# Weight chunks' loads in the opening wait for a one-word VectorE write to their buffer

## The chip, the cores and the metric

The kernel runs on one core of a Trainium2 chip. The metric is the device time of one execution in microseconds (us). A core has five engines that run their own instruction streams in order and wait for each other by semaphores: TensorE (PE; its weight loads are PEld), VectorE (DVE), ScalarE (ACT), GpSimd (POOL) and SyncE (SP), which here does nothing but issue transfers (DMAs).

## The reference

Three stages follow one another, all in float32. First a gated linear attention over 4 batches, 8 heads, 768 steps and 48 channels; then two MLPs over the 3072 tokens of 384 channels, each with a hidden layer of 2048.

```python
f = 1.0 / (1.0 + np.exp(-f_logit))
for t in range(S):
    state = f[:, :, t, :, None] * state + np.einsum('bhd,bhe->bhde', k[:, :, t], v[:, :, t])
    y[:, :, t] = np.einsum('bhd,bhde->bhe', q[:, :, t], state)
x = y.transpose(0, 2, 1, 3).reshape(B * S, H * D)
h = x @ moe_w_in;  g = np.maximum(h, 0.0) ** 2;  x = g @ moe_w_out
h = x @ moe2_w_in; g = h * np.tanh(softplus(h)); out = g @ moe2_w_out
```

## The kernel before

**Attention** is cut into 24 units, i = 0 to 23 (12 chunks of 64 steps, two pairs of batches each). A unit loads its gate logits, k and q (`load_j` and `load_f`, or `load_f` alone), and its v (`load_v`, two transfers), and passes through `v_min`, `a_exp`, `a_ln`, `v_scan`, `a_dq`, `a_dk`, `v_q`, `v_k`, `m_a`, `m_t`, `v_mask`, `a_kn`, `m_y`, `m_u`, `a_y`, `m_x`, `v_s`, `a_x`, `v_x`. The letter ahead of the underscore is the engine: `m` TensorE, `v` VectorE, `a` ScalarE, `load` SyncE. Four units make one block of 512 tokens for the MLPs.

**The first MLP** takes its hidden layer in 16 chunks. For block b and chunk fc, numbered i = 16 b + fc, `do_l1 i` makes the hidden values (9 matmuls, line 333), `act_a i` (ScalarE) and `act_b i` (VectorE, line 357) square and split them into a high part `gh` and a low part `gl`, and `do_l2 i` multiplies them back (9 matmuls, line 344). The second of the 9 matmuls of `do_l2` reads `gl`.

**Weights** are stored as 64-bit words and converted on the chip. Chunk fc of the first MLP (both of its matrices, 768 KB) is loaded by `load_w fc` into a buffer of its own (tag `w_fc`), and then goes through six steps: `w_abs` (ScalarE, line 251, the first to read the buffer), `w_shift` (VectorE, line 255), `w_top` (258), `w_low` (261), `w_hi` (ScalarE, 278) and `w_lo` (VectorE, 283). `do_l1 fc` needs what `w_hi` and `w_lo` wrote. The buffers of chunks 12 to 15 first serve as the inputs of units 5 to 2.

**The order** of the first part, up to the middle of `do_l1 18`, is written out in the string `START`; later steps are placed by the functions `unit`, `put` and `run`. Each engine runs its own steps in the order in which `START` names them, so the string is five queues in one. Warm-up matmuls (`m_warm`) keep TensorE busy in the opening. SyncE's queue before is, with j for `load_j`, f for `load_f`, v for `load_v`, w for `load_w`:

```
j0 j1 j2 j3 f0 f1 v0 w0 v1 f2 v2 f3 v3 w1 w2 w3 w4 f5 w5 w6 v4 w7 w8 w9 w11 f4 v5 f7 w10 f6 v7 w14 w12 w13 w15 v8 v6 f9 f8 v10 v9 f10
```

A transfer waits for the steps that still use its destination; the buffers of chunks 0 to 11 have no earlier user, so before the change their loads wait for nothing but their turn.

Of the kernel before, what the change touches and what calls it, by code (L numbers as in the profile page):

```python
# [35 lines left out]
START = """
m_warm 14; load_j 0; v_min 0; a_exp 0; load_j 1; load_j 2; load_j 3; a_ln 0; v_min 1; a_exp 1; v_scan 0; a_ln 1;
load_f 0; load_f 1; v_min 2; v_scan 1; a_dq 0; v_min 3; a_dk 0; v_k 0; a_exp 2; a_dq 1; v_q 0 1; v_q 0 0; a_dk 1;
load_v 0; load_w 0; a_ln 2; a_exp 3; eye_kn 0; load_v 1; load_f 2; m_t 0; m_warm 2; v_end 1; v_k 1; v_q 1 1;
load_v 2; v_scan 2; a_ln 3; load_f 3; v_end 0; v_q 1 0; m_a 0; m_warm 5; v_scan 3; v_mask 0 0; w_abs 0; v_mask 0 1;  # L40
m_a 1; m_warm 4; a_dq 2; a_dk 2; v_mask 1 1; load_v 3; a_dq 3; v_mask 1 0; m_y 0; a_kn 0; load_w 1; w_shift 0;
a_dk 3; v_q 2 0; m_t 1; m_warm 2; w_top 0; eye_kn 1; a_y 0; v_q 2 1; load_w 2; m_y 1; m_warm 3; a_y 1; v_q 3 0;
v_k 3; v_k 2; v_q 3 1; w_low 0; m_x 0; a_x 0; m_u 0; a_kn 1; v_s 0 0; m_a 2; w_abs 1; v_x 0; load_w 3; v_mask 2 0;
m_u 1; v_s 1 0; v_s 0 1; w_shift 1; m_a 3; m_t 3; v_mask 2 1; w_hi 0; a_kn 3; m_t 2; m_warm 1; m_y 2; a_kn 2;
v_s 1 1; v_mask 3 1; v_mask 3 0; m_x 1; m_warm 1; m_y 3; m_warm 1; w_lo 0; w_top 1; load_w 4; w_abs 2; a_x 1; v_x 1;
a_y 2; w_shift 2; m_x 2; load_f 5; a_y 3; w_low 1; a_x 2; load_w 5; m_x 3; m_warm 6; load_w 6; v_end 3; a_x 3; v_x 3;
v_x 2; w_top 2; do_l1 0; w_hi 1; w_abs 3; load_v 4; w_lo 1; w_low 2; do_l1 1; w_abs 4; w_shift 3; v_min 5; w_hi 2;
load_w 7; w_top 3; a_exp 5; w_lo 2; w_shift 4; m_u 3; load_w 8; w_low 3; act_a 0; act_b 0; w_abs 5; w_top 4; w_hi 3;
w_shift 5; load_w 9; do_l1 2; act_a 1; w_lo 3; w_low 4; w_hi 4; act_b 1; load_w 11; w_top 5; w_lo 4; w_low 5;
v_s 3 0; do_l2 0; do_l1 3; do_l2 1; act_a 2; act_b 2; do_l1 4; w_abs 6; w_hi 5; w_abs 7; w_shift 6; w_lo 5; w_top 6;  # L50
do_l2 2; act_a 3; w_abs 8; w_shift 7; w_low 6; load_f 4; a_ln 5; w_hi 6; w_top 7; act_b 3; v_s 3 1; act_a 4; w_lo 6;
w_abs 9; do_l1 5; do_l2 3; w_low 7; w_hi 7; load_v 5; act_b 4; w_shift 8; load_f 7; act_a 5; w_shift 9; load_w 10;
do_l1 6; w_top 8; load_f 6; do_l2 4; v_end 2; w_lo 7; w_top 9; w_low 8; act_b 5; act_a 6; w_hi 8; w_abs 11; v_min 4;
v_scan 5; w_lo 8; load_v 7; do_l1 7; w_low 9; load_w 14; a_exp 4; do_l2 5; a_ln 4; act_b 6; a_dq 5; w_hi 9; a_dk 5;
v_q 5 1; w_abs 10; w_lo 9; v_scan 4; do_l1 8; act_a 7; do_l2 6; v_k 5; a_dq 4; v_q 5 0; act_a 8; do_l1 9; a_dk 4;
w_shift 10; act_b 7; w_top 10; v_q 4 1; m_t 5; v_min 6; w_shift 11; v_k 4; act_a 9; act_b 8; m_a 5; load_w 12;
do_l2 7; v_min 7; m_u 2; v_q 4 0; do_l2 8; w_low 10; a_kn 5; m_a 4; w_top 11; m_t 4; a_exp 7; v_mask 5 0; w_hi 10;
a_ln 7; w_lo 10; v_end 5; v_end 4; w_low 11; act_b 9; w_abs 12; w_hi 11; w_shift 12; v_mask 5 1; w_top 12; do_l1 10;
do_l2 9; w_lo 11; act_a 10; do_l1 11; w_low 12; load_w 13; w_hi 12; w_abs 13; act_b 10; do_l2 10; v_mask 4 1;
w_lo 12; v_s 2 0; v_s 2 1; do_l1 12; act_a 11; w_shift 13; v_mask 4 0; w_abs 14; a_exp 6; act_b 11; m_y 5; a_ln 6;  # L60
w_top 13; w_shift 14; a_kn 4; do_l2 11; w_low 13; v_scan 6; w_hi 13; m_y 4; w_lo 13; a_y 5; act_a 12; do_l1 13;
v_scan 7; w_top 14; a_dq 7; act_b 12; a_dk 7; load_w 15; w_low 14; v_q 7 0; m_u 5; v_s 5 0; v_k 7; a_dq 6; v_q 7 1;
do_l2 12; act_a 13; m_u 4; a_dk 6; m_a 7; act_b 13; v_s 4 0; v_q 6 1; w_hi 14; v_q 6 0; do_l2 13; v_s 5 1; load_v 8;
v_k 6; a_y 4; v_s 4 1; v_mask 7 1; m_t 7; a_kn 7; w_abs 15; v_mask 7 0; m_a 6; v_mask 6 1; m_t 6; m_y 7; v_mask 6 0;
m_x 5; a_kn 6; load_v 6; a_x 5; m_x 4; m_y 6; a_y 7; a_x 4; w_lo 14; w_shift 15; do_l1 14; v_end 7; a_y 6; w_top 15;
w_low 15; v_x 5; load_f 9; w_hi 15; v_x 4; load_f 8; v_end 6; m_u 7; m_x 6; act_a 14; w_lo 15; m_u 6; v_s 7 0;
v_min 8; v_s 7 1; a_exp 8; v_min 9; do_l1 15; a_ln 8; m_x 7; a_x 6; act_b 14; a_x 7; v_scan 8; v_x 6; a_dq 8; v_x 7;
v_s 6 1; do_l2 14; a_dk 8; a_exp 9; v_s 6 0; v_k 8; act_a 15; v_q 8 0; act_b 15; a_ln 9; do_l1 16; v_scan 9; m_t 8;
v_end 8; act_a 16; load_v 10; do_l1 17; a_dq 9; v_q 8 1; v_q 9 0; v_end 9; a_dk 9; load_v 9; do_l2 15; a_kn 8;
v_q 9 1; do_l1 18; act_b 16; m_a 8; v_mask 8 1; v_mask 8 0; do_l2 16; m_y 8; m_u 8; act_a 17; a_y 8; load_f 10;  # L70
y_dma 8; act_b 17; v_k 9; v_s 8 0; v_s 8 1
"""
# [871 lines left out]
```

## Time and profile before

| | |
|---|---|
| runs | 898.8, 900.05, 900.1 us; median 900.05 us |
| profiled execution | 899.7 us, of which the span from first to last instruction is 897.9 us |
| granted TensorE clock | 0.998 of full speed |
| PE busy | 884.8 us, 99% of the span |
| DVE busy | 675.9 us, 75% |
| ACT busy | 618.5 us, 69% |
| first matmuls of `do_l1 0` without a gap | from 35.52 us |

Times in the rows below are us from the start of the span. The 1.8 us between span and execution lie outside the instructions. Granted clock 1.00 is the higher of the two levels, 2.4 GHz.

### The profile page before, as it was taken

Reading aid. Unit: us, or ns where it says so; the run is one execution under the profiler, and the core shown is the slowest. Engines: PE = TensorE matmul, PEld = TensorE weight load, DVE = VectorE, ACT = ScalarE, POOL = GpSimd, SP = SyncE. Lnnn points to the kernel's source line nnn. Section 1 sums busy time; section 2 is a strip of 40 time slices with the busy share of each in tenths; the row PEclk is TensorE's granted clock in tenths of the full one; section 3 lists DMA queues with packets and bytes.
Section 4 is the critical chain, followed back from the end, with each engine's and each line's share of the span. In section 5 each row is a group of like instructions: output and inputs, shape, how many; then the busy total and the mean of one; then the engine's idle time right before and its main releaser. Section 6 shows DMA issues by size and latency. Waiting matters only on the chain.

```text
span 897.9 us, 15329 instructions
## 1 busy us (share of the span) xinstructions
PE 884.8 (99%) x5927; PEld 726.5 (81%) x5927; DVE 675.9 (75%) x1146; ACT 618.5 (69%) x1131; POOL 5.3 (1%) x21
## 2 busy tenths in 40 slices
PE   8899999999999999999999999999999999999997
PEld 8788888888787887888888888888888888888885
DVE  8999976776778777772222788888788888888785
ACT  7898776876787678764544566666666676666664
POOL 2000000000000000000000000000000000000000
PEclk9999999999999999999999999999999999999999
DMA  9972223454536465622453200200100100200001
GB/s 244 351 172 106 82 89 100 152 186 157 187 126 228 135 195 165 221 101 81 175 200 118 71 0 1 72 1 0 71 1 1 71 0 1 72 1 0 36 1 38
DMA packets 34287, 89.93 MB, mean 100 GB/s; under 512 B 5216, under 2 KB 11360, under 8 KB 34208
## 3 DMA queue, kind: packets, MB, share of 16 engines
q1 hardware_dynamic: 34208, 88.89, 30.8%
q8 instruction: 48, 0.79, 0.4%
q14 instruction: 31, 0.25, 0.1%
HBM read 63.70 MB, written 22.02 MB: 95 GB/s over the span
## 4 chain that ended last, share of the span: by engine, by line
PE 87%; ACT 4%; DVE 3%; DMA 3%; SPq 2%; issue 1%; ACTq 0%
PE h L333 40%; PE a L344 40%; PE y L525 2%; DMA r<-in_w_dram 1%; DMA ax<-ay 1%; PE tr L486 1%; PE aq L471 1%; ACT r L716 1%; PE uq L538 1%; DMA sr<-in_w_dram 1%; PE u L543 1%; PE at L476 1%; PE y L518 0%; DMA vs<-in_vv_dram 0%; ACT r L715 0%
## 5 line engine op out<-in xcount | busy, mean ns | idle before, releaser
L333 PE MATMUL h<-x,w 128*128 128x512 f32 x1728 | 425.3, 390 | 0.4 <-DVE x L606 0.3
L344 PE MATMUL a<-gh,w 128*128 128x512 f32 x1146 | 388.3, 394 | 0.0
L333 PEld LDWEIGHTS h<-x,w 128*128 128x128 f32 x1728 | 323.6, 188 | 69.9 <-DVE x L606 1.0
L344 PEld LDWEIGHTS a<-gh,w 128*128 128x128 f32 x1146 | 215.2, 188 | 46.1
L344 PE MATMUL a<-gl,w 128*128 128x512 f32 x573 | 223.7, 391 | 0.0
L782 ACT ACTIVATE e<-e 128x512 f32<-128x512 f32 x95 | 60.1, 632 | 117.6 <-DVE e L781 117.6
L344 PEld LDWEIGHTS a<-gl,w 128*128 128x128 f32 x573 | 107.7, 188 | 22.0 <-DVE gl L357 0.7
L357 DVE TENSOR_TENSOR gl<-r,gh 128x512 fp32r<-128x512 f32 x96 | 65.8, 685 | 78.4 <-ACT gh L352 78.1
L781 DVE TENSOR_SCALAR e<-h 128x512 f32<-128x512 f32 x95 | 65.7, 692 | 60.7 <-PE h L333 58.1
L715 ACT ACTIVATE r<-h 128x512 f32<-128x512 f32 x96 | 56.6, 590 | 50.4 <-PE h L333 49.9
L776 ACT ACTIVATE r<-u,cst 128x512 f32<-128x512 f32 x94 | 67.9, 722 | 8.7 <-DVE u L790 2.7
L790 DVE SCALAR_TENSOR_TENSOR u<-e 128x512 f32<-128x512 f32 x95 | 65.9, 693 | 10.1 <-ACT e L782 0.7
L357 DVE TENSOR_TENSOR gl<-g,gh 128x512 fp32r<-128x512 f32 x95 | 65.7, 692 | 0.0
L778 DVE TENSOR_TENSOR e<-h,u 128x512 f32<-128x512 f32 x94 | 64.3, 684 | 0.0
L785 DVE TENSOR_TENSOR g<-e,r 128x512 f32<-128x512 f32 x94 | 64.2, 683 | 0.0
L716 ACT ACTIVATE r<-r 128x512 f32<-128x512 f32 x96 | 60.7, 632 | 3.1
L352 ACT ACTIVATE gh<-r 128x512 fp32r<-128x512 f32 x96 | 60.7, 632 | 3.1
L352 ACT ACTIVATE gh<-g 128x512 fp32r<-128x512 f32 x95 | 60.1, 633 | 3.1 <-DVE g L809 0.8
L777 ACT ACTIVATE r<-r 128x512 f32<-128x512 f32 x94 | 59.5, 633 | 3.0
L606 DVE TENSOR_TENSOR x<-ax,x 128x384 fp32r<-128x384 f32 x16 | 8.9, 555 | 35.3 <-ACT x L602 35.3
L602 ACT ACTIVATE x<-ax 128x384 fp32r<-128x384 f32 x16 | 8.4, 525 | 37.0 <-DMA ax<-ay 36.8
L508 ACT ACTIVATE kn<-tr 64x192 f32<-64x192 f32 x88 | 28.4, 322 | 6.1 <-PE tr L486 5.2
(120 smaller groups left out, 730.5 us busy)
## 6 DMA issues: line engine op xcount, KB each, us to landing
r<-in_w_dram SPq DMA_DIRECT2D x16, 768.0 KB, 11.7
sr<-in_w_dram SPq DMA_DIRECT2D x32, 384.0 KB, 3.5
w2d<-sw SPq DMA_DIRECT2D x32, 384.0 KB, 3.2
w<-w2d SPq DMA_DIRECT2D x32, 384.0 KB, 3.6
in<-in_qkf_dram SPq DMA_DIRECT2D x18, 672.0 KB, 5.8
vs<-in_vv_dram SPq DMA_DIRECT2D x48, 96.0 KB, 5.6
x2d<-ot SPq DMA_DIRECT2D x18, 256.0 KB, 2.2
x<-x2d SPq DMA_DIRECT2D x6, 768.0 KB, 5.1
```

The lines of the kernel that those rows point to most:

```text
L333: T.matmul(out=ps, lhsT=w[:, k * 128:(k + 1) * 128], rhs=x[:, s, k], start=(i == 0), stop=(i == 8))
L344: T.matmul(out=acc[m], lhsT=w[:, m * 128:(m + 1) * 128], rhs=gx, start=(fc == 0 and i == 0), stop=(fc == FC - 1 and i == 2))
L352: A.activation(out=gh, in_=g, func=AF.Copy)
L357: V.tensor_tensor(out=gl, in0=g, in1=gh.bitcast(F32), op=ALU.subtract)
L716: A.activation(out=r, in_=r, func=AF.Square)
L776: A.activation(out=r, in_=u, func=AF.Ln, bias=two)
L777: A.activation(out=r, in_=r, func=AF.Exp, scale=-1.0)
L778: V.tensor_tensor(out=e, in0=hp, in1=u, op=ALU.mult)
L781: V.tensor_scalar(out=e2, in0=ps, scalar1=20.0, scalar2=None, op0=ALU.min)
L782: A.activation(out=e2, in_=e2, func=AF.Exp)
L785: V.tensor_tensor(out=g, in0=e, in1=r, op=ALU.mult)
L790: V.scalar_tensor_tensor(out=u2, in0=e2, scalar=2.0, in1=e2, op0=ALU.add, op1=ALU.mult)
```

## The change

A new step `v_gate fc` allocates the buffer of chunk fc and writes one 32-bit word to it with a VectorE memset. `load_w fc` then takes that buffer, and since it writes over the same word it has to wait for the memset, that is, for VectorE to have come to that place of its queue. Chunks 1 to 11, 14 and 15 get a gate (13 memsets); 0, 12 and 13 don't. `START` is replaced. The queues of VectorE, ScalarE and TensorE name the same steps in the same order as before, but for the gates. SyncE's queue is another from `w1` on:

```
j0 j1 j2 j3 f0 f1 v0 w0 v1 f2 v2 f3 v3 w1 f5 w2 v4 w3 w4 f4 v5 f7 w5 f6 w6 w7 v7 w8 w9 w11 w10 w12 w14 w13 w15 v8 v6 f9 f8 v10 v9 f10
```

The places of the gates in VectorE's queue: gate 1 behind `v_scan 2`, 2 behind `w_shift 0`, 3 behind `w_low 0`, 4 behind `v_mask 2 0`, 5 behind `v_mask 3 0`, 6 behind `w_low 2`, 7 behind `w_top 3`, 8 behind `w_low 3`, 9 behind `act_b 1`, 11 behind `w_shift 7`, 10 behind `w_low 7`, 14 behind `w_top 11`, 15 behind `v_scan 7`. Five stand ahead of the last VectorE step that `do_l1 0` needs (`v_x 2`), eight ahead of `w_lo 3`, ten ahead of `act_b 3`.

```diff
 START = """
-m_warm 14; load_j 0; v_min 0; a_exp 0; load_j 1; load_j 2; load_j 3; a_ln 0; v_min 1; a_exp 1; v_scan 0; a_ln 1;
-load_f 0; load_f 1; v_min 2; v_scan 1; a_dq 0; v_min 3; a_dk 0; v_k 0; a_exp 2; a_dq 1; v_q 0 1; v_q 0 0; a_dk 1;
-load_v 0; load_w 0; a_ln 2; a_exp 3; eye_kn 0; load_v 1; load_f 2; m_t 0; m_warm 2; v_end 1; v_k 1; v_q 1 1;
...
-y_dma 8; act_b 17; v_k 9; v_s 8 0; v_s 8 1
+m_warm 14; load_j 0; load_j 1; load_j 2; load_j 3; load_f 0; v_min 0; load_f 1; a_exp 0; load_v 0; v_min 1; a_ln 0;
...
+eye_kn 0; v_q 1 1; v_scan 2; m_warm 5; v_end 1; a_ln 3; v_gate 1; load_w 1; v_q 1 0; v_end 0; v_scan 3; load_f 5;
+m_a 1; w_abs 0; v_mask 0 0; m_warm 4; a_dq 2; v_mask 0 1; a_dk 2; v_mask 1 1; m_y 0; a_dq 3; v_mask 1 0; a_kn 0;
+m_t 1; w_shift 0; m_warm 2; v_gate 2; load_w 2; v_q 2 0; a_dk 3; w_top 0; m_y 1; eye_kn 1; v_q 2 1; m_warm 3; a_y 0;
+v_q 3 0; a_y 1; v_k 3; m_x 0; m_u 0; v_k 2; a_x 0; a_kn 1; v_q 3 1; m_a 2; load_v 4; w_low 0; v_gate 3; load_w 3;
+m_u 1; v_s 0 0; w_abs 1; v_x 0; m_a 3; v_mask 2 0; v_gate 4; load_w 4; w_hi 0; v_s 1 0; m_t 3; v_s 0 1; load_f 4;
+a_kn 3; w_shift 1; m_t 2; load_v 5; v_mask 2 1; m_warm 1; v_s 1 1; m_y 2; a_kn 2; load_f 7; v_mask 3 1; m_x 1;
+v_mask 3 0; v_gate 5; load_w 5; m_warm 1; w_abs 2; load_f 6; w_lo 0; m_y 3; a_x 1; a_y 2; w_top 1; m_warm 1; a_y 3;
...
     def load_w(fc):
-        t = wp.tile([128, 2 * DM, 2], U32, tag=f"w_{fc}", name=f"r_{fc}", bufs=1)
+        t = raw.get(fc) or wp.tile([128, 2 * DM, 2], U32, tag=f"w_{fc}", name=f"r_{fc}", bufs=1)
         nc.sync.dma_start(out=t.rearrange("p c w -> p (c w)"), in_=w1[fc].bitcast(U32))
         raw[fc] = t
+
+    def v_gate(fc):
+        raw[fc] = wp.tile([128, 2 * DM, 2], U32, tag=f"w_{fc}", name=f"r_{fc}", bufs=1)
+        V.memset(raw[fc][0:1, 0:1, 0:1].bitcast(F32), 0.0)
```

## Rows read from the trace of the kernel before

**Rows 1.** The page: the chain that ended last, shares of the span.
```profile
PE 87%; ACT 4%; DVE 3%; DMA 3%; SPq 2%; issue 1%; ACTq 0%
```
**Rows 2.** Windows: length, busy time by engine, clock, DMA share, GB/s moved.
```profile
9.60:35.50 25.90, 22.58 (x409) 20.06 (x408) 25.45 (x39) 20.29 (x52) 0.00 (x0) 1.00 1.03 306
...
45.60:61.00 15.40, 15.40 (x68) 12.44 (x67) 15.31 (x23) 15.05 (x28) 0.00 (x0) 1.00 0.98 237
61.00:71.00 10.00, 10.00 (x45) 8.29 (x45) 9.94 (x14) 9.20 (x17) 0.00 (x0) 1.00 0.01 6
```
**Rows 3.** Groups by line, 16 to 140 us: w_abs of 15 chunks.
```profile
L251 ACT ACTIVATE wbit<-r 128x768 f32<-128x768 f32 x15 | 13.6, 906 | 0.9 <-DVE w L283 0.9
```
**Rows 4.** TensorE's timeline: matmuls of do_l1 0 and 1, gl's weight load in do_l2 3.
```profile
35.52 4.13 PE L333 MATMUL h<-x,w 128*128 128x512 f32 x17 [0.27 <-DVE x L606]
...
55.22 0.19 PEld L344 LDWEIGHTS a<-gl,w 128*128 128x128 f32 x1 [0.40 <-DVE gl L357]
```
**Rows 5.** VectorE's timeline: v_k 0; w_shift 0; act_b 0, w_top 4, w_shift 5, w_lo 3; act_b 3.
```profile
9.61 0.69 DVE L453 TENSOR_TENSOR in<-in,es 112x512 f32<-112x512 f32 x1 [1.09 <-DMA in<-in_qkf_dram]
...
18.57 0.54 DVE L255 TENSOR_SCALAR wbit<-wbit 128x768 uint32<-128x768 uint32 x1
...
41.88 0.67 DVE L357 TENSOR_TENSOR gl<-r,gh 128x512 fp32r<-128x512 f32 x1
42.48 0.94 DVE L258 SCALAR_TENSOR_TENSOR wbit<-r,wbit 128x768 uint32<-128x768 uint32 x1
43.35 0.54 DVE L255 TENSOR_SCALAR wbit<-wbit 128x768 uint32<-128x768 uint32 x1
43.82 0.94 DVE L283 SCALAR_TENSOR_TENSOR w<-wbit,w 128x768 fp32r<-128x768 f32 x1
...
54.48 0.69 DVE L357 TENSOR_TENSOR gl<-r,gh 128x512 fp32r<-128x512 f32 x1
```
**Rows 6.** w_low by its tile, 16 to 140 us: minimum, median, maximum in ns.
```profile
L261 DVE SCALAR_TENSOR_TENSOR wbit<-r,wbit x16: 939/942/959, 23.9 to 110.1; 128x768 uint32<-128x768 uint32 x16
```
**Rows 7.** VectorE's timeline at the start: memsets of one word in each partition.
```profile
1.70 0.06 DVE L622 MEMSET cst<- 112x1 f32 x1
1.82 0.06 DVE L623 MEMSET cst<- 32x1 f32 x1
```
**Rows 8.** SyncE's timeline, issues of w1, w4, f5, w5 and f4.
```profile
15.34 0.58 SPq L242 DMA_DIRECT2D r<-in_w_dram  x1
...
17.99 0.43 SPq L242 DMA_DIRECT2D r<-in_w_dram  x1
18.47 0.43 SPq L407 DMA_DIRECT2D early<-in_qkf_dram  x1
...
20.86 0.33 SPq L242 DMA_DIRECT2D r<-in_w_dram  x1
...
34.91 0.38 SPq L407 DMA_DIRECT2D early<-in_qkf_dram  x1
```
**Rows 9.** DMA issues of those stretches, w1, w4, f5, w5: us to landing last.
```profile
r<-in_w_dram SPq DMA_DIRECT2D x1, 768.0 KB, 7.8
...
r<-in_w_dram SPq DMA_DIRECT2D x1, 768.0 KB, 12.2
early<-in_qkf_dram SPq DMA_DIRECT2D x1, 672.0 KB, 14.8
...
r<-in_w_dram SPq DMA_DIRECT2D x1, 768.0 KB, 14.0
```
**Rows 10.** ScalarE's timeline: w_abs 5, w_hi 3, w_abs 7 and w_abs 8.
```profile
41.26 0.90 ACT L251 ACTIVATE wbit<-r 128x768 f32<-128x768 f32 x1
...
42.14 0.85 ACT L278 ACTIVATE w<-wbit 128x768 fp32r<-128x768 f32 x1
...
49.85 0.90 ACT L251 ACTIVATE wbit<-r 128x768 f32<-128x768 f32 x1
...
52.57 0.91 ACT L251 ACTIVATE wbit<-r 128x768 f32<-128x768 f32 x1
```

More of the change, by code (lines that the diff above doesn't have):

```diff
@@ L36 @@
 START = """
-m_warm 14; load_j 0; v_min 0; a_exp 0; load_j 1; load_j 2; load_j 3; a_ln 0; v_min 1; a_exp 1; v_scan 0; a_ln 1;
-load_f 0; load_f 1; v_min 2; v_scan 1; a_dq 0; v_min 3; a_dk 0; v_k 0; a_exp 2; a_dq 1; v_q 0 1; v_q 0 0; a_dk 1;
-load_v 0; load_w 0; a_ln 2; a_exp 3; eye_kn 0; load_v 1; load_f 2; m_t 0; m_warm 2; v_end 1; v_k 1; v_q 1 1;
-load_v 2; v_scan 2; a_ln 3; load_f 3; v_end 0; v_q 1 0; m_a 0; m_warm 5; v_scan 3; v_mask 0 0; w_abs 0; v_mask 0 1;
-m_a 1; m_warm 4; a_dq 2; a_dk 2; v_mask 1 1; load_v 3; a_dq 3; v_mask 1 0; m_y 0; a_kn 0; load_w 1; w_shift 0;
@@ L42 @@
[L42 to L70, printed above, removed]
-y_dma 8; act_b 17; v_k 9; v_s 8 0; v_s 8 1
+m_warm 14; load_j 0; load_j 1; load_j 2; load_j 3; load_f 0; v_min 0; load_f 1; a_exp 0; load_v 0; v_min 1; a_ln 0;
@@ new lines @@
+a_exp 1; v_scan 0; load_w 0; a_ln 1; load_v 1; v_min 2; a_dq 0; v_scan 1; load_f 2; a_dk 0; load_v 2; a_exp 2;
+v_min 3; v_k 0; a_dq 1; v_q 0 1; load_f 3; a_dk 1; m_t 0; v_q 0 0; a_ln 2; m_warm 2; load_v 3; v_k 1; a_exp 3; m_a 0;
+eye_kn 0; v_q 1 1; v_scan 2; m_warm 5; v_end 1; a_ln 3; v_gate 1; load_w 1; v_q 1 0; v_end 0; v_scan 3; load_f 5;
+m_a 1; w_abs 0; v_mask 0 0; m_warm 4; a_dq 2; v_mask 0 1; a_dk 2; v_mask 1 1; m_y 0; a_dq 3; v_mask 1 0; a_kn 0;
+m_t 1; w_shift 0; m_warm 2; v_gate 2; load_w 2; v_q 2 0; a_dk 3; w_top 0; m_y 1; eye_kn 1; v_q 2 1; m_warm 3; a_y 0;
@@ new lines @@
+v_q 3 0; a_y 1; v_k 3; m_x 0; m_u 0; v_k 2; a_x 0; a_kn 1; v_q 3 1; m_a 2; load_v 4; w_low 0; v_gate 3; load_w 3;
+m_u 1; v_s 0 0; w_abs 1; v_x 0; m_a 3; v_mask 2 0; v_gate 4; load_w 4; w_hi 0; v_s 1 0; m_t 3; v_s 0 1; load_f 4;
+a_kn 3; w_shift 1; m_t 2; load_v 5; v_mask 2 1; m_warm 1; v_s 1 1; m_y 2; a_kn 2; load_f 7; v_mask 3 1; m_x 1;
+v_mask 3 0; v_gate 5; load_w 5; m_warm 1; w_abs 2; load_f 6; w_lo 0; m_y 3; a_x 1; a_y 2; w_top 1; m_warm 1; a_y 3;
+m_x 2; v_x 1; w_shift 2; a_x 2; m_x 3; m_warm 6; v_end 3; w_low 1; a_x 3; v_x 3; w_hi 1; v_x 2; w_top 2; w_abs 3;
@@ new lines @@
+do_l1 0; w_lo 1; w_low 2; w_abs 4; v_gate 6; load_w 6; do_l1 1; w_shift 3; w_hi 2; v_min 5; w_top 3; a_exp 5;
+v_gate 7; load_w 7; act_a 0; w_lo 2; m_u 3; w_shift 4; do_l1 2; w_low 3; load_v 7; w_abs 5; v_gate 8; load_w 8;
+act_b 0; w_hi 3; w_top 4; do_l2 0; act_a 1; w_shift 5; w_lo 3; w_low 4; do_l1 3; act_b 1; w_hi 4; v_gate 9; load_w 9;
+w_top 5; act_a 2; do_l2 1; w_lo 4; w_low 5; w_abs 6; v_s 3 0; do_l1 4; w_hi 5; act_b 2; w_shift 6; w_abs 7; w_lo 5;
+act_a 3; do_l2 2; w_top 6; w_shift 7; v_gate 11; load_w 11; w_low 6; w_abs 8; do_l1 5; w_top 7; a_ln 5; w_hi 6;
@@ new lines @@
+act_b 3; v_s 3 1; do_l2 3; act_a 4; w_lo 6; w_low 7; v_gate 10; load_w 10; w_abs 9; do_l1 6; act_b 4; w_hi 7;
+w_shift 8; w_shift 9; act_a 5; w_top 8; do_l2 4; w_lo 7; v_end 2; w_top 9; act_a 6; do_l1 7; w_low 8; act_b 5;
+w_hi 8; v_min 4; v_scan 5; w_abs 11; do_l2 5; a_exp 4; w_lo 8; a_ln 4; w_low 9; do_l1 8; a_dq 5; act_b 6; w_hi 9;
+v_q 5 1; a_dk 5; w_lo 9; do_l2 6; w_abs 10; v_scan 4; act_a 7; v_k 5; do_l1 9; v_q 5 0; a_dq 4; w_shift 10; act_a 8;
+act_b 7; m_t 5; w_top 10; m_a 5; v_q 4 1; a_dk 4; v_min 6; do_l2 7; act_a 9; load_w 12; w_shift 11; v_k 4; act_b 8;
@@ new lines @@
+a_kn 5; v_min 7; m_u 2; v_q 4 0; w_low 10; do_l2 8; a_exp 7; w_top 11; w_hi 10; v_gate 14; load_w 14; v_mask 5 0;
+a_ln 7; m_a 4; w_lo 10; v_end 5; v_end 4; w_abs 12; w_low 11; m_t 4; do_l1 10; load_w 13; act_b 9; w_hi 11;
+w_shift 12; v_mask 5 1; do_l2 9; w_top 12; act_a 10; w_lo 11; w_low 12; do_l1 11; act_b 10; w_hi 12; v_mask 4 1;
+w_abs 13; w_lo 12; do_l2 10; act_a 11; v_s 2 0; v_s 2 1; w_shift 13; do_l1 12; w_abs 14; v_mask 4 0; act_b 11;
+a_exp 6; w_top 13; a_ln 6; m_y 5; a_kn 4; w_shift 14; w_low 13; do_l2 11; v_scan 6; w_hi 13; a_y 5; w_lo 13; m_y 4;
@@ new lines @@
+act_a 12; v_scan 7; do_l1 13; v_gate 15; load_w 15; w_top 14; a_dq 7; a_dk 7; act_b 12; m_u 5; a_dq 6; w_low 14;
+act_a 13; do_l2 12; v_q 7 0; v_s 5 0; v_k 7; a_dk 6; m_u 4; v_q 7 1; w_hi 14; act_b 13; m_a 7; a_y 4; load_v 8;
+v_s 4 0; v_q 6 1; do_l2 13; load_v 6; v_q 6 0; v_s 5 1; v_k 6; m_t 7; v_s 4 1; m_a 6; v_mask 7 1; a_kn 7; load_f 9;
+v_mask 7 0; m_t 6; v_mask 6 1; w_abs 15; m_y 7; load_f 8; v_mask 6 0; a_kn 6; m_x 5; m_x 4; w_lo 14; m_y 6;
+w_shift 15; a_x 5; do_l1 14; a_y 7; w_top 15; a_x 4; w_low 15; v_end 7; a_y 6; v_x 5; m_u 7; w_hi 15; v_x 4; v_end 6;
@@ new lines @@
+m_x 6; w_lo 15; act_a 14; m_u 6; v_s 7 0; do_l1 15; v_min 8; load_v 10; v_s 7 1; a_exp 8; v_min 9; a_ln 8; act_b 14;
+load_v 9; a_x 6; m_x 7; v_scan 8; do_l2 14; a_x 7; v_x 6; a_dq 8; v_x 7; a_dk 8; v_s 6 1; do_l1 16; a_exp 9; v_s 6 0;
+act_a 15; v_k 8; v_q 8 0; m_t 8; a_ln 9; do_l1 17; act_b 15; v_end 8; v_scan 9; act_a 16; v_q 8 1; do_l2 15; a_dq 9;
+v_end 9; v_q 9 0; a_dk 9; v_q 9 1; a_kn 8; do_l1 18; act_b 16; m_a 8; act_a 17; do_l2 16; v_mask 8 1; load_f 10;
+v_mask 8 0; act_b 17; m_y 8; v_k 9; m_u 8; a_y 8; y_dma 8; v_s 8 0; v_s 8 1
@@ L737, in attention @@
                m_x, y_dma, a_x, v_x, v_s, load_j, load_f, load_v, load_w, w_abs, w_shift, w_top, w_low, w_hi, w_lo, do_l1,
-               do_l2, act_a, act_b, m_warm, eye_kn)
+               do_l2, act_a, act_b, m_warm, v_gate, eye_kn)
         ops = {f.__name__: f for f in ops}
```

## The prediction

> **What bounds the kernel now.** I read the page first: TensorE is busy for 884.8 of 897.9 us (the table above) and makes 87% of the chain that ended last [rows 1]. So an edit counts only where TensorE doesn't run yet, or where it already waits. The timeline of TensorE shows where that is: its main work starts at 35.52 us, released by VectorE's last `v_x`, and from there on it runs nearly without a gap [rows 4]. I took the opening next. The windows show VectorE busy for 25.45 of the 25.90 us from 9.60 to 35.50 [rows 2], and its timeline has it waiting for a transfer for the last time at 9.61, for f0 [rows 5]. From there the opening is a queue of VectorE work, and its length sets the start of `do_l1 0`. VectorE stays full afterwards (15.31 of 15.40 us up to 61 us [rows 2]) because it converts the chunks just ahead of `do_l1`. One place shows that this queue still holds TensorE behind 35.52: the weight load for `gl` of `do_l2 3` waited 0.40 us, for the `act_b 3` that starts at 54.48 [rows 4, 5].
>
> The transfers come last. They are full too, a share of 1.03 up to 35.5 us and 0.98 from 45.6 to 61 [rows 2], but nobody waits for a weight chunk: behind 16 us `w_abs`, the first reader of a chunk, has 0.9 us of idle time ahead of it in 15 instances, and that was VectorE's doing [rows 3]. Chunks arrive in time already, and that decides what the change can win.
>
> **The change part by part.** *What it removes.* No wait on a transfer that bounds anything. The first 14 loads, j0 to w1, stand in the same order before and after, so f0 still releases VectorE at 9.61 and w0 and w1 land as before. VectorE, ScalarE and TensorE keep their orders. Gain: nothing.
>
> *The gates.* Each is one more instruction in a full VectorE queue. The trace has no one-word write between long steps, so I bound it. Low end: nothing, if it overlaps its neighbours whole. High end: 0.12 us, the distance from one such memset to the next (1.70 to 1.82) [rows 7]. Between them lies what a VectorE instruction costs apart from its elements: 512 elements took 0.60 us from start to start (41.88 to 42.48) and 768 took 0.87 (42.48 to 43.35) [rows 5]; 0.27 for 256 more elements leaves 0.06 for none, which is also a one-word memset's own duration [rows 7]. I take 0.06. With five gates ahead of `do_l1 0` this is 0.3 us, with eight ahead of `w_lo 3` 0.5, with ten ahead of `act_b 3` 0.6. Since TensorE waits for `act_b 3` already, those 0.6 us reach it whole; later gates (three) meet a TensorE that is that much later itself. The two ends give 0 and 1.2 us for ten.
>
> The Trainium skill (VectorE: DVE Perf Modes, the section on the TRN2 errata) puts the fixed term of a VectorE operation at about 150 cycles, where its table has 58. An estimate from these pages at 0.96 GHz is 0.16 us a gate by the first, 1.6 us for ten, and 0.06 by the second; the start-to-start rows above agree with the second, and the first returns among the rivals.
>
> *The order of the loads.* This is the larger question, since SyncE's new order puts f4, v5 and f7 ahead of w5, and f6 ahead of w6; all four stood behind w11 before. At most eight transfers seem to be under way: f4 was issued at 34.91 [rows 8], just as w5, the eighth issue before it, landed (20.86 + 14.0 = 34.9 [rows 8, 9]). They land one after the other. With a queue that never runs dry the order sets the landing times, not the gates; and it doesn't run dry after the change: gate 1 stands six steps of 0.6 us or more ahead of `w_shift 0` (18.57), so before w1's issue at 15.34, and gate 2, right behind `w_shift 0`, opens at some 19.2 us [rows 5, 8], with f3, v3, w1 and f5 still to land ahead of w2. So I add up landings. w1 lands at 15.34 + 7.8 = 23.14 and w4 at 17.99 + 12.2 = 30.19: w2, w3 and w4 took 7.05, 2.35 each. f5 landed at 18.47 + 14.8 = 33.27, 3.08 later; w5 at 34.86, only 1.6 later [rows 8, 9]. After the change there stand between w1 and w5: three f (f5, f4, f7), 9.24; w2 to w4, 7.05; v4 and v5, by bytes 192/768 of a chunk each, 1.2 together; and w5 itself, 1.6 to 2.35. So w5 lands between 42.2 and 43.0; I take 42.8, nearer the plain chunk.
>
> Who waits for it: `w_abs 5`, at 41.26 before [rows 10]. ScalarE comes there 0.3 us later now, and waits a good us. Behind it in ScalarE's queue stands `w_hi 3`, 0.88 us after the start of `w_abs 5` and 0.85 long (42.14 to 42.99 [rows 10]), and VectorE's `w_lo 3` needs that at 43.82 [rows 5]. The slack is 0.83; the eight gates add 0.5. A landing up to 41.26 + 0.83 + 0.48 = 42.57 therefore costs nothing; 42.8 costs 0.2 us, which VectorE carries to `act_b 3`. The next two stand about even: w7 lands at 42.8 + 3.1 (f6) + 2 x 2.35 = 50.6, and `w_abs 7` is due at 49.85 + 0.8; w8, behind v7, at 53.5, due at 52.57 + 0.8 [rows 10]. A wait of a few tenths there ends in work with more room. w12 to w15 have gates or other users long before their turn.
>
> The Trainium skill (DMA: Bandwidth & Descriptors, the section on the anatomy of one DMA) fits a transfer on its software path as 2 us plus bytes at 436 GB/s. By that estimate the 5.6 MB between w1 and w5 take 12.9 us, w5 lands at 36.0, and the sum is the gates alone. The trace disagrees: 306 GB/s from 9.6 to 35.5 us, 237 from 45.6 to 61 [rows 2].
>
> *The sum.* 0.6 (ten gates) + 0.2 (w5) = 0.8 us, on the profiled execution 899.7 + 0.8 = 900.5. That execution lies 0.35 below the median of the runs, so I forecast 900.9 us. If a gate costs less, w5 costs more (the slack shrinks by eight gates), so the sum hardly moves: with nothing a gate it is 0 + 0.7.
>
> **The rivals.** *1: the gates alone, hardly seen.* The gates change no landing that matters, and w5 comes by 42.2. For it: the queue is backlogged, and w5 followed f5 by 1.6 us. The time is that of ten gates, 0 to 0.6: 900.1 to 900.7, no difference that can be measured.
>
> *2: a gate costs the whole fixed part of an operation.* By durations, not starts, 0.67 us for 512 elements and 0.94 for 768 [rows 5] leave 0.13 with no elements. Ten then give 1.3 us; w5 has slack to 41.26 + 0.83 + 1.04 = 43.1 and costs nothing: 901.4. Against it: starts overlap that part. The errata section of the Trainium skill named above would have it so, at 901.6.
>
> *3: the chunks run late from w5 to w8.* In the stretch of before in which f loads stand among the chunks, 237 GB/s moved, so that 786 kB take 3.3 us [rows 2]. With 3.0 for each chunk behind w4, w5 lands at 43.5 (costs 0.9), w7 3.1 + 6.0 later at 52.6, and w8, behind v7, at 56.2: nearly 3 us behind `w_abs 8`'s turn at 53.4, and `act_a 4` waits behind it in ScalarE's queue. TensorE then runs out of `gh 4`: about 3 us, 903. It decides where a chunk behind w5 takes more than some 2.8 us.
>
> *4: faster.* The place is the VectorE queue of 25.9 us ahead of `do_l1 0`: if transfers that fill the memory slow VectorE's steps, fewer of them in the opening would shorten it. To win 1.8 us net, and 0.3 for five gates, steps must be 8% shorter: 898.2. Against it: the 16 `w_low` took 939 to 959 ns [rows 6], over stretches with a DMA share of 1.03 and of 0.01 [rows 2]; and the queue is no less full after the change.
>
> **How the numbers follow.** The forecast (0.5 to 1.6 us more, w5 a little late or not) gets 0.61, rival 1 0.15, rival 2 0.08, rival 3 0.12, rival 4 0.04. This kernel's runs lie within 0.15%, so about 0.2%, or 1.8 us, is the least that can be told from no change. The forecast, rivals 1 and 2 lie under it but for their upper tails (0.05): same 0.79, slower 0.12 + 0.05 = 0.17, faster 0.04. The range goes from no cost at all, on a median that falls 0.3 us low (899.8), to gates at 0.12 with w5 at 44.0: 1.2, and 44.0 - 43.05 = 0.95, 902.2, with 0.3 of scatter 902.5. It leaves out rivals 3 and 4.
>
> **What would show it.** After the change the first gapless matmul of `do_l1 0` stands 0.3 us later, near 35.8, and 13 new memsets of 0.06 us stand on VectorE. w5 lands near 42.8, `w_abs 5` waits for a transfer for about 1 us, and VectorE has a gap of some tenths ahead of `w_lo 3`. `act_b 3` starts near 55.3. From 60 us on the distance to the old timeline stays. The prediction is wrong if `do_l1 0` starts earlier, if `w_abs 6` to `8` wait more than 1 us each (rival 3), or if a wait appears behind 60 us, above all at chunks 12 to 15.

## The result, and the profile of the changed kernel

The changed kernel is slower: a median of 905.91 us (901.25 to 909.62, six runs) against 899.42 us (898.2 to 900.45, six runs), a ratio of 1.0071 with a 95% interval of 1.0054 to 1.0087. The forecast was 900.9 us, with a range up to 902.5. The profiled execution took 909.33 us, the second longest of its six, so what it shows is near the upper end of what the change costs.

The page of the changed kernel: TensorE's busy time, the chain that ended last, and the costliest group of matmuls, with the idle time ahead of it behind the last bar. From `w_abs` on, the lines of the changed file have numbers five higher than before (`do_l1` is L338, `w_abs` L256).

```profile
PE 886.4 (98%) x5927; PEld 727.1 (80%) x5927; DVE 677.2 (75%) x1159; ACT 618.4 (68%) x1131; POOL 5.2 (1%) x21
...
PE 85%; DMA 5%; ACT 4%; DVE 2%; SPq 1%; issue 1%; ACTq 0%
...
L338 PE MATMUL h<-x,w 128*128 128x512 f32 x1728 | 427.5, 392 | 5.3 <-ACT w L283 4.6
```

Against [rows 1] the share of transfers in the chain went from 3% to 5%, and of the 5.3 us that TensorE idles ahead of all `do_l1` matmuls, 4.6 are one wait for `w_hi` (L283). The view of waits (engine, line, what ended it: total us, times, longest) follows that wait back, first from 45 to 140 us, then from 16 to 45 us:

```profile
ACT wbit L256 <- DMA r<-in_w_dram: 5.8, 1, 5.8
DVE wbit L260 <- ACT wbit L256: 5.2, 1, 5.2
...
PE h L338 <- ACT w L283: 4.6, 1, 4.6
...
ACT wbit L256 <- DMA r<-in_w_dram: 5.2, 2, 3.6
...
PE at L482 <- issue: 1.3, 1, 1.3
```

One late chunk stops three engines in turn: `w_abs` waits 5.8 us for a transfer, VectorE 5.2 for `w_abs`, TensorE 4.6 for `w_hi`. Before, no transfer stood ahead of `w_abs` at all behind 16 us [rows 3]. The last line is another kind of wait: TensorE stood 1.3 us for nothing that the profile names. SyncE's timeline gives the start of the issues of w1 and w5, and the view of DMA issues, cut to each of them, the us to landing:

```profile
17.56 0.45 SPq L243 DMA_DIRECT2D r<-in_w_dram  x1
...
33.09 0.35 SPq L243 DMA_DIRECT2D r<-in_w_dram  x1
```
```profile
r<-in_w_dram SPq DMA_DIRECT2D x1, 768.0 KB, 9.5
...
r<-in_w_dram SPq DMA_DIRECT2D x1, 768.0 KB, 17.0
```

w1 lands at 27.1 (23.14 before [rows 8, 9]) and w5 at 50.1, where 42.8 was predicted: 4.0 us of the difference stand ahead of w1's landing, 3.3 between w1 and w5. The timelines of TensorE and ScalarE show what follows, in order of time: the unnamed wait in `m_a 3`, `do_l1 0` and `1`, `w_abs 5`, `do_l1 3`, the next `do_l1`, and the first matmul of `m_a 5`.

```profile
29.25 0.21 PE L482 MATMUL at<-mv,early 48*64 48x64 f32 x1 [1.32 <-issue]
...
37.20 4.73 PE L338 MATMUL h<-x,w 128*128 128x512 f32 x18
...
50.20 0.89 ACT L256 ACTIVATE wbit<-r 128x768 f32<-128x768 f32 x1 [5.77 <-DMA r<-in_w_dram]
...
51.97 4.35 PE L338 MATMUL h<-x,w 128*128 128x512 f32 x9 [4.64 <-ACT w L283]
...
58.30 2.20 PE L338 MATMUL h<-x,w 128*128 128x512 f32 x9
...
81.23 0.27 PE L481 MATMUL at<-mv,early 48*64 48x64 f32 x1
```

The windows (length, busy time by engine, granted clock, DMA share, GB/s) of the same stretch:

```profile
45.00:50.00 5.00, 2.33 (x10) 1.43 (x8) 1.02 (x2) 0.00 (x0) 0.00 (x0) 0.95 1.01 242
50.00:60.00 10.00, 8.03 (x26) 6.22 (x27) 8.55 (x13) 9.56 (x17) 0.00 (x0) 0.68 0.82 271
```

The transfers are as full as ever (1.01) and move 242 GB/s while ScalarE does nothing at all for 5 us. Behind the wait the granted clock is 0.68: a mean of the lower level, 1.2 GHz, and the higher, 2.4. `do_l1 3` took 4.35 us there, and an undisturbed one 2.20.

The same marks of the kernel before, on TensorE's timeline (`do_l1 3`, the next `do_l1`, first matmul of `m_a 5`):

```profile
44.66 2.20 PE L333 MATMUL h<-x,w 128*128 128x512 f32 x9
...
48.74 2.20 PE L333 MATMUL h<-x,w 128*128 128x512 f32 x9
...
71.97 0.27 PE L476 MATMUL at<-mv,early 48*64 48x64 f32 x1
```

Now the loss can be added up. The first 18 `do_l1` matmuls end at 37.20 + 4.73 = 41.93, before at 35.52 + 4.13 = 39.65 [rows 4]: 2.28. The wait: 4.64. From `do_l1 3` to the next `do_l1` 58.30 - 51.97 = 6.33 against 48.74 - 44.66 = 4.08: 2.25, the clock. Together 9.17, and the mark at `m_a 5` stands 81.23 - 71.97 = 9.26 later. The spans differ by 9.7, so nearly all of it is lost ahead of 81 us. That the 2.25 us are the clock's is tested below, in experiment 4.

### The profile page after: what moved, and what is told of

It is laid out like the page before. It is cut to its first block, busy times and chain, and to the rows that moved or that the text cites. A ratio compares the mean times of both kernels' runs of the same rounds, so it can differ in the third digit from the quotient of the medians.

```text
span 907.6 us, 15353 instructions
## 1 busy us (share of the span) xinstructions
PE 886.4 (98%) x5927; PEld 727.1 (80%) x5927; DVE 677.2 (75%) x1159; ACT 618.4 (68%) x1131; POOL 5.2 (1%) x21
## 4 chain that ended last, share of the span: by engine, by line
PE 85%; DMA 5%; ACT 4%; DVE 2%; SPq 1%; issue 1%; ACTq 0%
PE h L338 40%; PE a L349 40%; DMA r<-in_w_dram 3%; PE y L530 2%; DMA vs<-in_vv_dram 1%; DMA ax<-ay 1%; PE tr L491 1%; PE aq L476 1%; PE uq L543 1%; PE at L481 1%; DMA sr<-in_w_dram 1%; PE u L548 1%; ACT r L721 0%; PE y L523 0%; ACT r L720 0%
## 5 line engine op out<-in xcount | busy, mean ns | idle before, releaser
L338 PE MATMUL h<-x,w 128*128 128x512 f32 x1728 | 427.5, 392 | 5.3 <-ACT w L283 4.6
L338 PEld LDWEIGHTS h<-x,w 128*128 128x128 f32 x1728 | 324.6, 188 | 75.6 <-ACT w L283 5.1
```

Of the source, the lines that this page charges most:

```text
L338: T.matmul(out=ps, lhsT=w[:, k * 128:(k + 1) * 128], rhs=x[:, s, k], start=(i == 0), stop=(i == 8))
```

## The experiments

The theory after the result: the order of SyncE's queue brings w5 late and disturbs the opening; the gates themselves are free. The rival: the gates cost it, by their writes or because a load that waits for VectorE starts too late.

### 1. The order without the gates, the gates without the order, the writes alone

`order_only` takes the 13 `v_gate` out of the changed kernel. `gates_only` puts them into the old order (a load that would stand ahead of its own gate is moved right behind it: w6 to w9, w11 and w14). `writes_only` is the kernel before with 13 one-word writes at those places, to a tile that nobody reads.

```diff
 # order_only
-a_ln 3; v_gate 1; load_w 1; v_q 1 0; v_end 0; ...
+a_ln 3; load_w 1; v_q 1 0; v_end 0; ...
 # gates_only
-load_v 2; v_scan 2; a_ln 3; ...
+load_v 2; v_scan 2; v_gate 1; a_ln 3; ...
 # writes_only
+    def v_gate(fc):
+        V.memset(spare[0:1, 0:1], 0.0)
```

> The new SyncE order without any gate. Theory A (the order: f4, v5, f7 and f6 ahead of w5 to w9 use up the slack of the chunks): as slow as the changed kernel, 4 to 9 us over the kernel before, varying from execution to execution, w5 landing some 22 us behind w1 and w_abs 5 waiting several us for it. Theory B (the gates: loads are issued late and too few are under way): within 0.5 us of the kernel before, w5 landing near 35 to 40 us. The gates' own cost on VectorE (0.6 us) falls away in both.

> All 13 gates at their places, but SyncE's order of the kernel before up to v7 (f4, v5, f7 and f6 behind w11). Theory A: the gates' writes alone, 0.3 to 0.9 us over the kernel before, little scatter, no wait of w_abs 5 to 8 above 0.5 us. Theory B: as slow as the changed kernel, 4 to 9 us over, with w5 to w8 issued at their gates and landing after their turn.

> The kernel before with 13 one-word VectorE writes to a spare word at the gates' places; no load waits for them and SyncE's order is that of before. Both theories: the price of the writes alone, 0.6 us over the kernel before (0 to 1.2); do_l1 0 starts 0.3 us later. If it is above 1.5 us, a write costs more than its 0.06 us and the gates matter by themselves.

Measured: `order_only` 905.47 us, ratio 1.0063 [1.0049, 1.0078]; `gates_only` 900.07, 1.0003 [0.9994, 1.0012]; `writes_only` 900.14, 1.0002 [0.9993, 1.0011]. By the ratios the order alone costs 5.7 us of the 6.4 that the changed kernel lost, and the two intervals overlap; the gates cost 0.2 to 0.3 us, not to be told from nothing. In the changed kernel VectorE's timeline shows why: a gate of 0.06 us starts while the step ahead of it still runs (`w_low 0`, gate 3, the next step).

```profile
25.51 0.94 DVE L266 SCALAR_TENSOR_TENSOR wbit<-r,wbit 128x768 uint32<-128x768 uint32 x1
26.39 0.06 DVE L248 MEMSET r<- 1x1 f32 x1
26.50 0.56 DVE L597 TENSOR_TENSOR vs<-u,f 48x384 f32<-48x384 f32 x1
```

The profiled execution of `order_only` (904.83 us) loses its time at another place than that of the changed kernel did. TensorE's timeline (the unnamed wait in `m_a 3`, `do_l1 0` and `1`, `m_a 5`) and two windows:

```profile
27.98 0.21 PE L481 MATMUL at<-mv,early 48*64 48x64 f32 x1 [1.41 <-issue]
...
39.87 4.47 PE L337 MATMUL h<-x,w 128*128 128x512 f32 x18
...
76.51 0.27 PE L480 MATMUL at<-mv,early 48*64 48x64 f32 x1
```
```profile
30.00:32.00 2.00, 1.51 (x28) 1.51 (x29) 1.99 (x3) 1.89 (x7) 0.00 (x0) 0.50 1.00 358
...
36.00:38.00 2.00, 2.00 (x11) 2.00 (x11) 0.00 (x0) 1.15 (x5) 0.00 (x0) 0.50 1.03 217
```

TensorE is busy for 2.00 of 2.00 us, but at 0.50, 1.2 GHz, from 30 to 40 us; `do_l1 0` and `1` end at 44.34, 4.69 late, and `m_a 5` is 4.54 late. So time is lost at two places, in the opening and at w5, and an execution shows more of the one or of the other.

### 2. The changed kernel again

No edit; the profile of another execution.

> The changed kernel once more, to see how its executions differ: 901 to 910 us. If the landings scatter (Theory A with a rate that differs from execution to execution), w1 lands anywhere between 23 and 27 us and w5 20 to 23 us behind it, and the wait of w_abs 5 follows w5's landing one to one. If w5 lands at the same time in a slower and a faster execution, something else makes the difference.

Measured: 906.37 us, 1.0075 [1.005, 1.0099]; profiled at 903.84. w1 landed at 22.3 and w5 at 45.5, 23.1 behind it; `w_abs 5` waited 1.5 us; TensorE's unnamed wait in `m_a 3` was 2.00 us and the clock 0.50 from 28 to 34, and `do_l1 0` came at 37.65. The distance from w1 to w5 repeats (23.0 in the first profile, 23.1 here, 21.4 in `order_only`). The wait of `w_abs 5` was longest where w1 landed last: 5.77 us with w1 at 27.1, 1.4 and 1.5 with w1 at 25 (`order_only`) and at 22.3. With three profiles that is an indication, no more.

### 3. One part of the order at a time

`f5_first` moves f5 alone ahead of w2. `f467_first` leaves f5 and moves v4, f4, v5, f7 ahead of w5 and f6 ahead of w6. Neither has gates.

```
before      w1 w2 w3 w4 f5 w5 w6 v4 w7 w8 w9 w11 f4 v5 f7 w10 f6 v7 ...
f5_first    w1 f5 w2 w3 w4 w5 w6 v4 w7 w8 w9 w11 f4 v5 f7 w10 f6 v7 ...
f467_first  w1 w2 w3 w4 f5 v4 f4 v5 f7 w5 f6 w6 w7 v7 w8 w9 w11 w10 ...
```

> The kernel before with one move in SyncE's queue: f5 goes out ahead of w2 instead of behind w4; no gates. In the runs with the new order do_l1 0 began 1.7 to 4.4 us late, behind a wait of TensorE inside m_a 3 that ended on nothing but instruction issue (1.3 to 2.0 us). Theory A1 (f5 in flight at 22 to 28 us holds up TensorE's instruction transfer and w2): that wait appears here too, do_l1 0 begins 1 to 4 us late and the time is 2 to 4 us over the kernel before. Theory A2 (only f4, v5, f7 and f6 ahead of w5 matter): within 0.5 us of the kernel before.

> The rest of the new order: w1 to w4 and f5 as before, then v4, f4, v5, f7 ahead of w5 and f6 ahead of w6; no gates. Theory A2: w5 lands 20 to 23 us behind w1, w_abs 5 waits for it, and the time is 2 to 6 us over the kernel before, with do_l1 0 at its old time (35.5). Theory A1: do_l1 0 at its old time too, and what is left is what w5's lateness costs, under 2 us.

> f5 ahead of w2 once more (898.9 to 906.1 in 12 executions; the profiled one was the fastest). In a slower execution: a wait inside m_a 3 of 1.3 to 2.0 us that ends on instruction issue, the instruction transfer taken up later than at 23.5 us, and a granted clock of 0.5 for some us behind it, as in the new order. If instead w1 or w2 is late and the clock stays, the instruction transfer isn't the cause.

Measured: `f5_first` 901.79 us, 1.0031 [1.0019, 1.0044], from 898.92 to 906.14 in twelve runs; again 902.56, 1.0033 [1.002, 1.0046]. `f467_first` 905.06, 1.0058 [1.0045, 1.0071]. Its waits from 16 to 60 us, its timeline (end of the opening, `do_l1 3`, the next `do_l1`, `m_a 5`) and windows:

```profile
ACT wbit L251 <- DMA r<-in_w_dram: 8.0, 2, 5.4
DVE wbit L255 <- ACT wbit L251: 4.3, 1, 4.3
```
```profile
35.67 4.15 PE L333 MATMUL h<-x,w 128*128 128x512 f32 x17 [0.28 <-DVE x L606]
...
48.63 4.35 PE L333 MATMUL h<-x,w 128*128 128x512 f32 x9 [3.65 <-ACT w L278]
...
55.59 2.20 PE L333 MATMUL h<-x,w 128*128 128x512 f32 x9
...
78.51 0.27 PE L476 MATMUL at<-mv,early 48*64 48x64 f32 x1
```
```profile
50.00:52.00 2.00, 2.00 (x6) 1.52 (x6) 2.00 (x4) 1.89 (x4) 0.00 (x0) 0.50 1.01 299
...
54.00:56.00 2.00, 2.00 (x9) 1.64 (x8) 1.97 (x4) 2.00 (x5) 0.00 (x0) 0.91 1.02 388
```

With f5 in its old place the opening ends as before (39.82 against 39.65), and the loss stands wholly at w5, which lands at 46.8, 23.5 behind w1: 0.17, the wait of 3.65, and 55.59 - 48.63 - 4.08 = 2.88 at the lower clock make 6.70; `m_a 5` is 6.54 late. So v4, f4, v5 and f7 ahead of w5 are the larger part, 5.2 us by the ratio. f5 ahead of w2 is the smaller, some 2 to 3 us. The parts don't add up: the whole order costs 5.7. Both profiles of `f5_first` fell on the shortest run of their set (898.92 and 900.37), so where its longer runs lose their time is not shown; an unnamed wait of 0.9 and 1.5 us in `m_a 3` stands in both, at clock 1.00.

### 4. What the clock costs

`f467_fill` is `f467_first` with 14 spare matmuls ahead of `do_l1 3`, which write a tile that nobody reads and fill TensorE's wait.

```diff
-do_l2 0; do_l1 3; do_l2 1; ...
+do_l2 0; m_fill 14; do_l1 3; do_l2 1; ...
+        def m_fill(n):
+            sm = cap.rearrange("p h t -> p (h t)")
+            t = h_p.tile([128, 512], F32, tag="h", name="fill")
+            for _ in range(n):
+                T.matmul(out=t[:, 0:128], lhsT=sm[:, 0:128], rhs=sm[:, 0:128])
```

> The order with f4, v5, f7 ahead of w5 (905.06 before), with 14 matmuls into a spare PSUM tile ahead of do_l1 3, where TensorE waited 3.65 us for w_hi 3 and then ran do_l1 3 in 4.14 us instead of 2.04 and do_l2 1 in 2.8 instead of 2.04 at a granted clock of 0.50. They fill some 3.2 us of the wait. If that part of the loss is the clock's, it stays at 1.00 and the time falls by 2 to 3 us, to 902.5; if not, the time stays or grows.

Measured: 902.82 us, 1.0036 [1.0022, 1.005], 2.2 us under `f467_first`, although the spare matmuls add work. TensorE's timeline: the spare matmuls (two records each), `do_l1 3` in two pieces, `m_a 5`.

```profile
45.09 3.29 PE L619 MATMUL fill<-cap 112*128 112x128 f32 x28
48.13 0.71 PE L333 MATMUL h<-x,w 128*128 128x512 f32 x2
49.06 1.87 PE L333 MATMUL h<-x,w 128*128 128x512 f32 x7 [0.22 <-DVE w L283]
...
76.25 0.27 PE L476 MATMUL at<-mv,early 48*64 48x64 f32 x1
```

`do_l1 3` starts 0.5 us earlier than in the profile of `f467_first`, since w5 landed 0.6 earlier, and runs at clock 1.00; from its start to the next `do_l1` it is 4.7 us where it was 7.0. `m_a 5` is 4.28 late where it was 6.54. So of the loss at w5 some 2.2 us is the clock and the rest the late chunk. This execution (905.62 us, the longest of its six) lost 1.8 us more near 238 us, in another wait with no named cause, which `f467_first` doesn't show.

### 5. The rows of an f load

One pair of rows of the kernel before, which the prediction did not use, compares the two kinds of load. Behind 70 us the queue is no longer full. A weight chunk issued at 73.21 and an f issued at 128.31, us to landing:

```profile
r<-in_w_dram SPq DMA_DIRECT2D x1, 768.0 KB, 4.0
...
in<-in_qkf_dram SPq DMA_DIRECT2D x1, 672.0 KB, 4.8
```

An f has an eighth less bytes than a chunk and takes 0.8 us longer here. It fills 112 partitions, a chunk 128. So f's were loaded with 128 rows, the last 16 of them zeros that nobody reads (`rows128`), and with 120 (`rows120`), in the new order without gates, in the old order, and in the changed kernel whole.

```diff
-        inp = [at1.tile([112, 3, 512], F32, name=f"in{i}") for i in range(2)]
+        inp = [at1.tile([128, 3, 512], F32, name=f"in{i}") for i in range(2)]
...
-            return [t[:, j] for j in range(3)]
+            return [t[0:112, j] for j in range(3)]
...
-    qkf = np.zeros((NC, 2, 112, 3, H * C), a.dtype)
+    qkf = np.zeros((NC, 2, 128, 3, H * C), a.dtype)
```

> The new order without gates, as before measured at 905.5, with the units' inputs stored and loaded with 128 rows instead of 112 (the 16 more rows are zeros that nothing reads; an f load is then 768 KB, as a weight chunk). If the 112 rows make an f load slow (672 KB alone took 4.8 us where 768 KB of weights took 4.0 to 4.4), f5 lands within 2.5 us of w1, w5 within 19 us of w1, and the time falls by 2 us or more. If an f load is slow for its place or its source, it grows by its bytes: w5 lands a further 1 to 2 us late.

> The kernel before with the same 128 rows. If 112 rows are what is slow, f0 lands up to 1 us earlier than at 9.5 and the opening, a queue of VectorE work from there on, ends up to 1 us earlier: 899 us. If bytes decide, f0 lands 1 us later and the time is 1 us over.

> The changed kernel, gates and order, with 128 rows in the units' inputs instead of 112 and nothing else. Theory C (the new order costs only because a 112-row f load is slow and slows what lands beside it): the loss is gone, 898.5 to 900.0 us, scatter under 2 us, w5 landing some 16 to 17 us behind w1. Theory A (the order by itself): still 3 us or more over the kernel before.

> The new order without gates, with 120 rows (8 rows of zeros more than 112): does the row count or something of 128 make the loads quick? If it is 128 alone, as a full set of partitions: near 905.5, as with 112 rows. If any multiple of 8 above 112 does: near 898.9, as with 128 rows. In between if the rate grows by steps.

| | median, us | ratio to before |
|---|---|---|
| new order, 112 rows (`order_only`) | 905.47 | 1.0063 [1.0049, 1.0078] |
| new order, 120 rows | 907.22 | 1.0086 [1.0067, 1.0105] |
| new order, 128 rows | 898.9 | 0.9991 [0.9982, 1.0] |
| old order, 128 rows | 899.02 | 0.999 [0.9981, 0.9998] |
| changed kernel, 128 rows | 899.47 | 1.0 [0.9991, 1.0008] |

The new order with 128 rows: windows, and the us to landing of w5, which was issued at 28.28.

```profile
23.00:35.00 12.00, 10.53 (x197) 9.12 (x197) 11.79 (x20) 9.04 (x24) 0.00 (x0) 1.00 1.01 334
35.00:45.00 10.00, 10.00 (x72) 8.09 (x73) 10.00 (x15) 8.20 (x15) 0.00 (x0) 1.00 1.03 378
```
```profile
r<-in_w_dram SPq DMA_DIRECT2D x1, 768.0 KB, 11.1
```

w5 lands at 39.4, 16.3 behind w1 at 23.1, though more bytes lie between. By landings its three f took 6.7 us together and its four chunks 7.9, against 8.9 and 10.5 in `order_only`. The changed kernel moved, in the same two windows, with the DMA share as full:

```profile
23.00:35.00 12.00, 9.09 (x212) 8.05 (x212) 11.45 (x21) 8.49 (x26) 0.00 (x0) 1.00 1.03 287
...
35.00:45.00 10.00, 9.90 (x80) 7.79 (x78) 9.68 (x18) 7.20 (x16) 0.00 (x0) 1.00 1.02 225
```

In these windows `order_only` moved 284 and 234 GB/s, and the changed kernel with 128 rows 325 and 377.

Two things follow. A DMA share of 1.0 says that the engines are occupied, not that they move much: 225 and 378 GB/s stand beside 1.02 and 1.03. And f loads of 112 rows, when several of them are under way, slow the chunks beside them too. With 128 rows the order costs nothing, with gates or without. 120 rows don't help: w5 lands at 49.4 there, and `w_abs` waits 10.9 us in four places.

Alone, the rows make less of a difference than the pair above suggests. The same f with 128 rows, issued at 128.81 in `rows128_old_order`:

```profile
in<-in_qkf_dram SPq DMA_DIRECT2D x1, 768.0 KB, 4.5
```

Over the profiles this f took 4.6 to 4.8 us with 112 rows, 4.4 to 4.5 with 128 and 5.6 with 120, and the first lone chunk 3.9 to 4.4. So a lone f gains 0.1 to 0.4 us by the padding, and in the full queue 0.8 for each f and 0.6 for each chunk beside it.

The Trainium skill (DMA: Bandwidth & Descriptors, the section on why a DMA increments its semaphore by 16) says that a transfer is shared out over the largest number of DMA engines, up to 16, that divides the outermost dimension of its source and of its destination, here the rows. That gives 16 engines for 112 and for 128 rows and 15 for 120, so by that rule the number of engines can't be what parts 112 from 128. The same page (The descriptor swizzle) says that in a transfer of 128 rows each engine writes its own one of 16 memory ports; it doesn't say what happens with 112, and no run here shows the ports. Why 112 and 120 rows are slow stays open. The padding also changes how far apart the f's lie in memory (128 rows of 6 KB instead of 112); no run changes the one without the other.

The old order with 128 rows is about 0.9 us under the kernel before (the interval reaches from 0.2 to 1.7), and so is the new order with 128 rows. That is at the edge of what can be measured. The expected reason, f0 landing earlier and a shorter opening, isn't seen: in the profile f0 landed at 9.9 (9.5 before) and `do_l1 0` came at 35.98 (35.52).

## Why the prediction was wrong

The step that failed is "The order of the loads": it let w5 land at 42.8 and cost 0.2 us, and it let w0 and w1 land as before. In the first profile w5 landed at 50.1, the wait and the lower clock behind it cost 6.9 us, and the opening another 2.3. The structure held: a queue that never runs dry, landings one after the other, and, where w5 is waited for, `w_abs 5`, `w_hi 3` and `do_l1 3` behind it. The sizes did not hold, and two terms, the clock and the opening, were missing.

**The price of a chunk.** 2.35 us came from w2, w3 and w4, which follow each other in the old queue with f5 behind them. In the new queue f's stand among them. From w1 to w5 the changed kernel took 23.0 us, predicted 19.7. By landings the three f took 3.49, 2.88 and 2.68, together 9.05 (predicted 9.24), v4 and v5 1.64 (1.2), but the four chunks 1.95, 3.00, 3.98 and 3.41, together 12.34 (9.4 at most). So the price of an f was right and that of a chunk beside f's was too low. The row for it was at hand, 237 GB/s in the stretch where f's stand among chunks [rows 2], but it went into rival 3 only: 3.3 us a chunk at that rate, and 3.1 was measured on average. w4 came late in this profile too: it landed at 40.26, and `w_abs 4` began at 40.34, 0.9 us behind the `w_lo 1` that it followed at once before. The profile puts that wait down to the gate of chunk 6, which `w_abs 4` doesn't need. With 128 rows, where f's and chunks took 2.2 and 2.0 each, the forecast's price would have been high enough.

**Where the count starts.** "w0 and w1 land as before" held in some executions only: w1 landed at 22.3 to 27.1 us in those of the new order that were profiled. In the two profiles of the changed kernel w0, which stands ahead of the first moved load, landed at 16.9 and 13.2 (14.8 before). So landings of one kernel scatter by some us between executions. The runs of the changed kernel spread over 8.4 us and those of the kernel before over 2.3. That the old order hides the scatter, since its chunks have room, fits but isn't shown: the kernel before was profiled once.

**What a late chunk costs.** The sum let lateness reach TensorE one for one beyond the slack. A wait of 3.65 or 4.64 us also drops the granted clock, which adds 2.2 us (shown by the spare matmuls). That term was not in the sum. The Trainium skill (TensorE: Matmul & The Clock Gate, the section on HAM oscillation) has this case, a matmul loop that waits for a transfer and goes on at half the clock. The traces agree: 0.50 behind the wait, 1.00 with the spare matmuls.

**The opening.** The forecast moved `do_l1 0` by the gates alone, to about 35.8. It came at 37.20, 37.65 and 39.87 in the three profiles of the new order with 112 rows. What stands ahead of it there is the unnamed wait in `m_a 3`, in two of the three the lower clock behind it, and in two of the three waits of `w_abs 0` and `1` for w0 and w1: 5.2 us together in the first profile, 3.3 in `order_only`, none in the second profile of the changed kernel. The kernel before had 2.0 us of this, ahead of 16 us, where the prediction didn't look:

```profile
14.83 0.92 ACT L251 ACTIVATE wbit<-r 128x768 f32<-128x768 f32 x1 [1.96 <-DMA r<-in_w_dram]
```

These were no term at all. How much of the delay each brings wasn't parted. In the changed kernel with 128 rows the wait in `m_a 3` is 0.9 us, the clock stays at 1.00 and `do_l1 0` comes at 34.75.

**The gates.** 0.6 us was forecast, 0.3 measured, with an interval of -0.5 to 1.1. Rival 2's 1.3 us lies outside it. With the new order the gates add 0.4 to 0.9 us by medians (`order_only` against the two sets of the changed kernel) and 0.6 with 128 rows, which would fit the forecast's term, but these intervals overlap. That the gates change no landing that matters held too: `gates_only` moves its loads later and less densely and loses nothing.

**The rivals.** Rival 3 named the right chunk and the right sign, but not the right way: its 3.0 us a chunk was to make w7 and w8 late one after the other, and in the changed kernel no chunk behind w5 is waited for. Its 903 us was still 3 us low, for want of the clock and the opening. Rival 4 didn't occur. That the distance from 60 us on stays was right (9.3 us at 81, 9.7 at the end).

## What to carry to other kernels

When a change reorders transfers in a full queue, price each by rows in which the same kinds lie side by side, read the GB/s and not the DMA share, and try a shape in the full queue: alone, 112 rows looked at most a few tenths of a us worse than 128. Ask how far the landings scatter between executions before counting a few tenths of slack, and add to a wait of TensorE of some us (3.65 and 4.64 here) the time at the lower clock that followed it, 2.2 to 2.9 us. Where a load can be padded to 128 rows, try that before tuning the order; here it took away the whole loss.

## What the runs showed of the hardware

- In the full queue f loads of 128 rows with 14% more bytes landed faster than those of 112, and so did the chunks beside them: 334 and 378 GB/s against 284 and 234 (new order without gates), and 16.3 us from w1 to w5 against 21.4 to 23.5.
- In the profiles of the new order with 112 rows one packet of instructions (0.02 MB, 1.1 to 1.3 us long) starts between 25.1 and 26.4 us, and TensorE waits 1.3 to 2.0 us for nothing named, always ahead of the same matmul of `m_a 3`. Before, the packet starts at 23.6, and there is no such wait. In all eight profiles that have the wait it ends 1.2 to 1.6 us behind the packet's end, and in the other six TensorE comes to that matmul 1.3 to 1.9 us behind it and doesn't wait. So the packet may well be what TensorE waits for, but it was not isolated. `gates_only` has an unnamed wait of 1.9 us too, without a loss, but ahead of `m_a 2` and ended before its packet had landed: another wait.
- Behind that wait the granted clock fell to 0.50 in two of three profiles, for 6 to 10 us, though TensorE had not stood for more than 2.0 us at a time there; in the third, with 1.3 us, it stayed at 1.00.
